# Phase one of a fused attention and MLP kernel: first norms deferred, fewer transposes on TensorE, x loads and attention outputs moved

## The chip, the cores and the metric

The kernel runs on one core of one Trainium2 chip. The metric is the device time of one execution in microseconds (us), as the median of several runs. Experiments ran beside runs of the kernel before. A ratio is the mean time of one kernel's fast runs over that of the other's fast runs of the same rounds, so it is not quite the ratio of the medians quoted. A profile is one execution; its span lies about 2 us below the time of the run it was taken in.

## The reference, cut to what matters

The input x is 2048 rows of 1024 values in bf16. It is normalised once, and two branches take the result: a memory-augmented attention (not touched here, apart from one number) and a mixer with an MLP.

```python
xn = _layernorm(x)                       # "first norm"
out = x + A(xn, ...) + B(xn, ...)
# B starts with a second norm of the same rows and a matmul:
h  = _gelu(_layernorm(xn) @ w1)          # phase one of the kernel
x1 = xn + shift(h) @ w2                  # phase two
h2 = _gelu(_layernorm(x1) @ w3) @ w4     # phase three
```

## The kernel before

Phase one works on 16 tiles of 128 rows. For each tile it needs the statistics of x (`norm_stats`: VectorE, then an inverse root on POOL, called the factor below), the second norm `xn2` (computed straight from x, bf16), its transpose `xn2T`, eight groups of matmuls with w1 (`stage1`), and a gelu on ScalarE per group. A group writes one of four PSUM buffers, and its gelu frees that buffer for a later group. The first norm `xn` is needed only later, by phase two and by the attention; it is kept in SBUF and also written to a scratch in HBM.

The order within each engine is the order of the program text; the PE timeline of the profile before shows it in tile 0's stage: six groups of eight matmuls from 8.38 us, half of tile 1's transpose at 11.77 us, one group at 12.06 us, the other half at 12.51 us. Tiles 0 to 7 are transposed by TensorE (matmuls with the identity, copied out of PSUM by ScalarE); tiles 8 to 15 are normalised on ScalarE and transposed by DMA. The core of the code, cut:

```python
NPE = 8
def norm2(n, xn2T, jj):
    ...
    if n < NPE:                                  # VectorE
        nc.vector.tensor_scalar(xn2, xts[n], mean, rstd2, op0=subtract, op1=mult)
    else:                                        # ScalarE, then a DMA transpose
        nc.scalar.activation(xn2, xts[n], Identity, bias=nm2, scale=rstd2)
        nc.sync.dma_start_transpose(xn2T[:, jj], xn2)

def norm1(n):                                    # first norm, and its write
    nc.vector.tensor_scalar(xn, xts[n], mean, rstd1, op0=subtract, op1=mult)
    nc.gpsimd.dma_start(xn_v[:, n, :], xn)       # to the scratch in HBM
    load_x(n + 10)                               # ten x buffers
    ...
for n in range(1, NPE):
    norm_stats(n + 1, 0); norm2_of(n); norm_stats(n + 1, 1)
    if n > 1: norm1(n - 2)                       # two tiles behind
    if n < 4: stage1(n - 1, 1, ..., transposes of tile n after groups 5 and 6)
...
def prep(n):                                     # tiles 8 to 15, inside stage1
    norm2_of(n); norm_stats(n + 1); norm1(n - 2)
for n0 in range(4, NT, 2):                       # two tiles at a time
    stage1(n0, 2, tiles2[n0], between)           # 256 columns per matmul
```

In the attention the outputs of a tile are put in the order of the program 12 us (in block 0) or 10 us (in blocks 1 to 4) of estimated TensorE time after its scores.

Of the kernel before, what the change touches and what calls it, by code (L numbers as in the profile page):

```python
# [15 lines left out]
BF16 = mybir.dt.bfloat16  # L16
F32 = mybir.dt.float32
# [6 lines left out]
P = 128  # L24
S = 2048
D = 1024
KT = D // P
NT = S // P
# [49 lines left out]
def kernel(  # L78
# [114 lines left out]
    with tc.manual_schedule(engines={mybir.EngineType.PE, mybir.EngineType.SP, mybir.EngineType.Pool}), ExitStack() as actx:  # L193
# [6 lines left out]
        with ExitStack() as bctx:  # L200
# [13 lines left out]
            with ExitStack() as hctx:  # L214
# [7 lines left out]
                with ExitStack() as p0:  # L222
                    big = p0.enter_context(tc.tile_pool(name="p0big", bufs=1))
                    ring = p0.enter_context(tc.tile_pool(name="p0ring", bufs=3))
                    w1_sb = big.tile([P, KT, D], BF16)
                    NPE = 8

                    xts = {}

                    def load_x(n):  # L230
                        if n < NT:
                            xts[n] = ring.tile([P, D], BF16, tag="xt", bufs=10, name=f"xt{n}")
                            nc.sync.dma_start(xts[n][:], x_v[:, n, :])

                    load_x(0)
# [5 lines left out]
                        load_x(n)  # L241
                    for i in range(4):
                        nc.sync.dma_start(w2_sb[:, 2 * i:2 * i + 2, :], w2_v[:, 2 * i:2 * i + 2, :])
                    for n in range(7, 10):
                        load_x(n)

                    stats = {}

                    def norm_stats(n, part=None):

                        if n >= NT:
                            return
                        xt = xts[n]
                        if n not in stats:
                            stats[n] = [ring.tile(shape, F32, tag=tag, bufs=6, name=f"{tag}{n}") for tag, shape in (("st", [P, 2, 6]), ("mv", [P, 2]), ("ab", [P, 2]), ("rr", [P, 2]), ("nm2", [P, 1]))]
                        st, mv, ab, rr, nm2 = stats[n]
                        if part in (None, 0):
                            nc.vector.bn_stats(st[:, 0, :], xt[:, 0:512])
                        if part == 0:
                            return  # L260
                        nc.vector.bn_stats(st[:, 1, :], xt[:, 512:1024])
                        nc.vector.bn_aggr(mv[:], st[:])
                        nc.vector.scalar_tensor_tensor(ab[:], epsm[:], mv[:, 1:2], epsa[:], op0=ALU.mult, op1=ALU.add)
                        nc.gpsimd.tensor_tensor(rr[:], ab[:], neghalf[:], op=ALU.pow)
                        if n >= NPE:
                            nc.gpsimd.tensor_scalar(nm2[:], mv[:, 0:1], rr[:, 1:2], -1.0, op0=ALU.mult, op1=ALU.mult)

                    def norm2(n, xn2T, jj):
                        st, mv, ab, rr, nm2 = stats[n]
                        xn2 = ring.tile([P, D], BF16, tag="xn2")  # L270
                        if n < NPE:
                            for c in (slice(0, 512), slice(512, 1024)) if n == 0 else (slice(0, 1024),):
                                nc.vector.tensor_scalar(xn2[:, c], xts[n][:, c], mv[:, 0:1], rr[:, 1:2], op0=ALU.subtract, op1=ALU.mult)
                        else:
                            nc.scalar.activation(xn2[:], xts[n][:], ACTF.Identity, bias=nm2[:], scale=rr[:, 1:2])
                            nc.sync.dma_start_transpose(xn2T[:, jj], xn2[:])
                        return xn2

                    def norm1(n):
                        st, mv, ab, rr, nm2 = stats[n]  # L280
                        xn = xn_keep[n // 4][:, n % 4]
                        nc.vector.tensor_scalar(xn, xts[n][:], mv[:, 0:1], rr[:, 0:1], op0=ALU.subtract, op1=ALU.mult)
                        nc.gpsimd.dma_start(xn_v[:, n, :], xn)
                        load_x(n + 10)
                        if n in (12, 15):
                            load_w3()
                        return xn
# [10 lines left out]
                    def stage1(n0, nt, xn2T, between, j0=0):  # L298
                        w = nt * P
                        for co in range(KT):  # L300
                            ps = psum.tile([P, 512], F32, tag="mm", bufs=4)
                            for k in range(KT):
                                nc.tensor.matmul(ps[:, :w].rearrange("p (n t) -> p n t", t=P), w1_sb[:, k, co * P:(co + 1) * P],  # L303
                                                 xn2T[:, j0:j0 + nt, k, :], start=(k == 0), stop=(k == KT - 1))
                            nc.scalar.activation(hTB[:, co, 2 + n0 * P:2 + n0 * P + w], ps[:, :w], ACTF.Gelu_apprx_tanh)
                            for f in between.get(co, ()):
                                f()
# [13 lines left out]
                    tiles2, xn2s = {}, {}  # L321

                    def norm2_of(n):
                        if n % 2 == 0:
                            tiles2[n] = xn2T_tile()
                        xn2s[n] = norm2(n, tiles2[n - n % 2], n % 2)

                    def tr(n, half, on_dve=False):
                        transposes(xn2s[n], tiles2[n - n % 2], n % 2, half, on_dve)
# [6 lines left out]
                    nc.gpsimd.memset(hTB[:, :, 0:2], 0.0)  # L336
                    nc.gpsimd.memset(hTB[:, :, S + 2:S + 4], 0.0)
                    load_consts(4)
                    for n in range(1, NPE):
                        if n > 1:  # L340
                            norm_stats(n + 1, 0)
                        norm2_of(n)
                        norm_stats(n + 1, 1 if n > 1 else None)
                        if n > 1:
                            norm1(n - 2)
                        if n < 4:
                            stage1(n - 1, 1, tiles2[(n - 1) // 2 * 2], {5: [lambda n=n: tr(n, 0)], 6: [lambda n=n: tr(n, 1)]}, (n - 1) % 2)
                    stage1(3, 1, tiles2[2], {4: [lambda: tr(4, 0)], 5: [lambda: tr(4, 1)], 6: [lambda: tr(5, 0)], 7: [lambda: tr(5, 1)]}, 1)

                    def prep(n):  # L350
                        norm2_of(n)
                        norm_stats(n + 1)
                        norm1(n - 2)

                    for n0 in range(4, NT, 2):
                        between = {c: [] for c in range(KT)}
                        if n0 + 4 < NT:
                            between[1 + 2 * (n0 == 4)] += [lambda n0=n0: prep(n0 + 4)]
                            between[4 + 2 * (n0 == 4)] += [lambda n0=n0: prep(n0 + 5)]
                        if n0 == 4:  # L360
                            for c in range(4):
                                between[1 + 2 * c // 2 + (c > 1)] += [lambda c=c: tr(6 + c // 2, c % 2)]
                        stage1(n0, 2, tiles2[n0], between)
                    for n in (NT - 2, NT - 1):
                        norm1(n)

                xn3T = [wpool.tile([P, 4, KT, P], BF16, tag="w", name=f"xn3T{tb}") for tb in range(4)]
                with ExitStack() as p2:
                    ring = p2.enter_context(tc.tile_pool(name="p2ring", bufs=4))
                    for n in range(NT):  # L370
                        x1 = ring.tile([P, D], F32, tag="x1")
                        st = ring.tile([P, 2, 6], F32, tag="st")
# [7 lines left out]
                        mv = ring.tile([P, 2], F32, tag="mv")  # L380
# [14 lines left out]
            with ExitStack() as p3:  # L395
# [3 lines left out]
                ring = p3.enter_context(tc.tile_pool(name="p3ring", bufs=2))  # L399
# [114 lines left out]
                for tb in range(4):  # L514
# [18 lines left out]
                    for j in range(4):  # L533
                        n = tb * 4 + j
# [223 lines left out]
        for gi_, group in enumerate(groups):  # L758
# [3 lines left out]
            for hg in range(8):  # L762
# [26 lines left out]
                for i, (B, t, QT, KTt, V) in enumerate(work):  # L789
                    due = clock[0] + 1.0 + i * step  # L790
                    if B["b"] not in oXs:
                        oXs[B["b"]] = oX_last if B["b"] == 4 else [abig.tile([P, H, 384], BF16, tag="oX", name=f"oX{B['b']}")]
                        if B["b"] == 3:
                            oXs[3].append(abig.tile([P, H, P], BF16, tag="oXb", name="oXb"))
                        oX_last = oXs[B["b"]]
                    j, at = divmod(480 if t["gi"] == 21 else t["tok"], 384)
                    oX = oXs[B["b"]][j]

                    def s_item(t=t, hg=hg, QT=QT, KTt=KTt, V=V, oX=oX, at=at, due=due, gi_=gi_):
                        PTr = scores(t, hg, QT, KTt)  # L800

                        def o_item():
                            outputs(t, hg, PTr, V, oX, at)
                            return 0.18
                        smalls.append((clock[0] + (12.0 if gi_ == 0 else 10.0), ("O", gi_), o_item))
                        return 0.18
                    smalls.append((due, ("S", gi_), s_item))
            outs = [Out(oXs[B["b"]], 3 * B["b"] + gl, gl, ch * 512) for B in Bs for gl in range(4 if B["b"] == 4 else 3) for ch in range(2)]
# [187 lines left out]
```

## Time and profile before

The median was 1521.8 us of 3 runs.

| what (profile before) | value |
|---|---|
| span | 1519.6 us |
| TensorE (PE) busy | 1508.8 us, 99% |
| TensorE waiting, all waits named | under 4 us |
| first matmul of phase two (L377) | at 69.39 us |
| granted TensorE clock | 1.00 from 6.9 us to 0.6 us before the end of the span |

First the page of the kernel before: the line of PE in the table of engines (busy time, share of the span, instructions), and the chain that ended last by engine.

```profile
PE 1508.8 (99%) x9781; PEld 808.3 (53%) x9853; DVE 546.2 (36%) x1137; ACT 506.7 (33%) x1147; POOL 179.4 (12%) x248
...
PE 98%; DMA 1%; issue 0%; DVE 0%; ACT 0%; SPq 0%; POOL 0%
```

Next all waits of PE in the kernel before: who waited for whom, us in total, how often, the longest.

```profile
PE warm L320 <- DVE wz L314: 1.4, 1, 1.4
PE ps L303 <- ACT xn2T L296: 0.5, 1, 0.5
PE psO L690 <- DMA PT<-Pn: 0.4, 1, 0.4
PE ps L292 <- DVE xn L273: 0.4, 1, 0.4
PE ps L651 <- DMA wt<-in_A_Wq_dram: 0.3, 1, 0.3
PE pso L709 <- issue: 0.2, 1, 0.2
```

There is hardly anything to win but TensorE's own instructions. No matmul of phase one waits for a DMA transpose (xn2T from DMA is not among the releasers; the one such wait, PT in the attention, is 0.4 us). The third view is the timeline of PE in phase one (start, duration, engine, line, operation, count):

```profile
32.49 0.39 PE L292 MATMUL ps<-c_ident_sb,xn 128*128 128x128 bf16 x4
32.71 36.84 PE L303 MATMUL ps<-xn2T,w_sb 128*128 128x256 bf16 x336
69.39 10.96 PE L377 MATMUL ps<-w_sb,hTB 128*128 128x512 bf16 x49
```

After the last transpose on TensorE (L292) phase one runs without a gap, 109 ns per matmul of 256 columns, until phase two begins.

### The profile page before, as it was taken

To read this page: it belongs to the slowest core of one execution; us is meant where nothing else is said; L and a number is where in the kernel's file an instruction comes from. 1 tells how busy PE (TensorE), PEld (TensorE's weight loads), DVE (VectorE), ACT (ScalarE), POOL (GpSimd) and SP (SyncE) were. 2 spreads that over 40 slices of the span, in tenths; PEclk is the share of its full clock that TensorE was granted. 3 is DMA by queue.
4 is the path that set the end of the run, shared out by engine and by line. 5 is a ranking of instruction groups with operands and counts; after the bars stand their busy time and mean duration, and the time that the engine had idled before them with its cause. 6 is when DMAs were issued, how large, how long until landed. Compare 5 with 4: busy or idle time off the path is not lost.

```text
span 1519.6 us, 24277 instructions
## 1 busy us (share of the span) xinstructions
PE 1508.8 (99%) x9781; PEld 808.3 (53%) x9853; DVE 546.2 (36%) x1137; ACT 506.7 (33%) x1147; POOL 179.4 (12%) x248
## 2 busy tenths in 40 slices
PE   9999999999999999999999999999999999999998
PEld 7844444445444444444466645654665555445555
DVE  7382230100120122222246614651664266416542
ACT  6533203013022011111256614650663266326630
POOL 5231020211111231100000010001000100010001
PEclk9999999999999999999999999999999999999999
DMA  8799762353355887532499947992997389628611
GB/s 283 157 266 317 220 174 93 136 201 111 126 169 141 198 281 255 192 133 70 137 240 253 238 117 189 244 238 79 228 240 190 118 223 217 185 76 209 175 46 53
DMA packets 306459, 274.20 MB, mean 180 GB/s; under 512 B 153787, under 2 KB 274128, under 8 KB 306088
## 3 DMA queue, kind: packets, MB, share of 16 engines
q1 hardware_dynamic: 284168, 189.92, 49.3%
q0 software_dynamic: 22032, 82.63, 15.9%
q8 instruction: 79, 1.29, 0.4%
q14 instruction: 36, 0.29, 0.1%
q10 hardware_dynamic: 144, 0.07, 0.0%
HBM read 190.98 MB, written 46.19 MB: 156 GB/s over the span
## 4 chain that ended last, share of the span: by engine, by line
PE 98%; DMA 1%; issue 0%; DVE 0%; ACT 0%; SPq 0%; POOL 0%
PE ps L651 30%; PE pso L709 14%; PE ps L577 14%; PE ps L519 13%; PE ps L545 13%; PE ps L377 4%; PE ps L303 3%; PE psS L666 2%; PE psO L690 2%; PE ps L836 1%; PE ps L469 1%; PE ps L434 0%; PE gps L448 0%; DMA wt<-in_A_Wq_dram 0%; DMA PT<-Pn 0%; PE warm L320 0%
## 5 line engine op out<-in xcount | busy, mean ns | idle before, releaser
L651 PE MATMUL ps<-hTb,wt 128*128 128x396 bf16 (+3 forms) x2528 | 500.4, 343 | 0.3 <-DMA wt<-in_A_Wq_dram 0.3
L651 PEld LDWEIGHTS <-wt 128*128 128x128 bf16 x2528 | 232.2, 98 | 167.6 <-DMA wt<-in_A_Wq_dram 0.7
L577 PE MATMUL ps<-wt,xT 128*128 128x512 bf16 x1003 | 220.1, 379 | 1.1
L709 PE MATMUL pso<-wo_sb,oX 128*128 128x512 bf16 x938 | 209.3, 379 | 1.2 <-issue 0.2
L519 PE MATMUL ps<-xn3T,w_sb 128*128 128x512 bf16 x896 | 196.2, 379 | 0.0
L545 PE MATMUL ps<-w_sb,h3T 128*128 128x512 bf16 x873 | 194.3, 379 | 1.2
L577 PEld LDWEIGHTS <-xT 128*128 128x128 bf16 x1024 | 100.2, 98 | 120.8
L520 ACT ACTIVATE h3T<-ps 128x512 bf16<-128x512 f32 x112 | 66.9, 597 | 290.4 <-PE ps L519 289.5
L709 PEld LDWEIGHTS <-oX 128*128 128x128 bf16 x960 | 92.6, 98 | 108.2
L657 ACT CAST KT<-ps 128x396 bf16<-128x396 f32 (+3 forms) x160 | 82.3, 514 | 186.9 <-PE ps L651 184.2
L545 PEld LDWEIGHTS <-h3T 128*128 128x128 bf16 x896 | 87.0, 98 | 103.4
L519 PEld LDWEIGHTS <-w_sb 128*128 128x128 bf16 x896 | 86.6, 98 | 102.1
L672 DVE TENSOR_REDUCE sums<-sm 99x4 f32<-99x396 f32 (+2 forms) x176 | 97.6, 555 | 113.0 <-ACT sm L670 113.0
L659 ACT ACTIVATE QT<-ps 128x396 bf16<-128x396 f32 (+3 forms) x160 | 84.2, 527 | 119.1 <-PE ps L651 102.0
L668 DVE TENSOR_TENSOR sm<-psS,c_mask_reg_sb 99x396 f32<-99x396 f32 x160 | 91.3, 571 | 86.3 <-PE psS L666 85.7
L579 ACT CAST Vs<-ps 128x512 bf16<-128x512 f32 x64 | 37.5, 587 | 233.1 <-PE ps L577 174.9
L670 ACT ACTIVATE sm<-sm 99x396 f32<-99x396 f32 (+2 forms) x176 | 92.9, 528 | 63.7 <-DVE sm L668 60.7
L583 DVE CAST Vs<-ps 128x512 bf16<-128x512 f32 x64 | 44.3, 692 | 170.0 <-PE ps L577 158.0
L678 DVE TENSOR_TENSOR Pn<-sm,rs 99x396 bf16<-99x396 f32 (+2 forms) x176 | 99.0, 562 | 7.2 <-DMA PT<-Pn 1.1
L546 DVE TENSOR_TENSOR R<-ps,R 128x512 f32<-128x512 f32 x32 | 21.9, 690 | 180.9 <-PE ps L545 166.6
L716 POOL DMA_DIRECT2D out_dram<-ot x30 | 16.4, 547 | 584.0 <-DVE ot L715 578.2
L715 DVE TENSOR_TENSOR ot<-pso,Rt 128x512 bf16<-128x512 f32 (+1 forms) x33 | 22.3, 676 | 172.3 <-PE pso L709 166.9
(120 smaller groups left out, 1072.0 us busy)
## 6 DMA issues: line engine op xcount, KB each, us to landing
wt<-in_A_Wq_dram SPq DMA_DIRECT2D x76, 512.0 KB
wt<-in_A_Wk_dram SPq DMA_DIRECT2D x76, 512.0 KB
wt<-in_A_Wv_dram POOLq DMA_DIRECT2D x24, 1024.0 KB, 6.5
V_scratch<-Vs SPq DMA_DIRECT2D x32, 512.0 KB
V<-V_scratch SPq DMA_DIRECT2D x32, 384.0 KB
R_scratch<-x POOLq DMA_DIRECT2D x16, 512.0 KB, 3.9
R<-R_scratch SPq DMA_DIRECT2D x16, 512.0 KB
R_scratch<-R POOLq DMA_DIRECT2D x16, 512.0 KB, 3.2
```

The lines of the kernel that those rows point to most:

```text
L519: nc.tensor.matmul(ps[:].rearrange("p (n t) -> p n t", t=P), w3_sb[:, k, f * P:(f + 1) * P], xn3T[tb][:, :, k, :], start=(k == 0), stop=(k ...
L520: nc.scalar.activation(h3T[:, f, :], ps[:], ACTF.Gelu_apprx_tanh)
L545: nc.tensor.matmul(ps[:], h3T[:, f, j * P:(j + 1) * P], w4_sb[:, f, ch * 512:(ch + 1) * 512], start=(f == 0), stop=(f == FT - 1))
L577: nc.tensor.matmul(ps[:], xT[:, m4 * 4 + j, k, :], wv[:, k, :], start=(k == 0), stop=(k == KT - 1))
L651: nc.tensor.matmul(ps[:, :nb] if flat else ps[:, :nb].rearrange("p (t c) -> p t c", t=nt), w[:, k, hh * P:(hh + 1) * P], B["rhs"](k), star ...
L657: nc.scalar.copy(o, i)
L659: nc.scalar.mul(o, i, scale)
L668: nc.vector.tensor_tensor(sm[:T, :, :T], S3, t["mask"][:].unsqueeze(1).to_broadcast((T, 4, T)), op=ALU.add)
L670: nc.scalar.activation(e[:T, :, :T], sm[:T, :, :T], ACTF.Exp, scale=LN2)
L672: nc.vector.tensor_reduce(ss, e[:T, :, :T], axis=AX.X, op=ALU.add)
L678: nc.vector.tensor_tensor(Pn[:T, :, :T], e[:T, :, :T], rs[:T, :].unsqueeze(2).to_broadcast((T, 4, T)), op=ALU.mult)
L709: nc.tensor.matmul(self.ps[:, :self.w], self.oX[self.gl // 3][:, h, self.gl % 3 * P:(self.gl % 3 + 1) * P], wo_sb[:, h, self.cc], start=(h ...
```

## The change

The intent: less work for TensorE (only tiles 0 to 4 are transposed there; 5 to 7 go to the DMA), earlier second norms for that (the first norms are put off and then done two per tile), x loads that are put off and issued together, ahead of the next tile's second norm and transpose, instead of one behind each first norm (and nine x buffers instead of ten, which leaves room for statistics that live longer), and outputs at 12 us in all blocks of the attention. The diff, cut to its core:

```diff
-                    NPE = 8
+                    NPE, NDVE = 5, 8
-            xts[n] = ring.tile([P, D], BF16, tag="xt", bufs=10, name=f"xt{n}")
+            xts[n] = ring.tile([P, D], BF16, tag="xt", bufs=9, name=f"xt{n}")
-                    for n in range(7, 10):
+                    for n in range(7, 9):
                         load_x(n)
 ...   # statistics: bufs=6 -> bufs=12; norm2 on VectorE for n < NDVE, DMA transpose for n >= NPE
                         nc.gpsimd.dma_start(xn_v[:, n, :], xn)
-                        load_x(n + 10)
+                        x_due.append(n + 9)
 ...
+                    def s_and_n(n):
+                        norm_stats(n + 1, 0); norm2_of(n); norm_stats(n + 1, 1)
+                    def more_x():
+                        while x_due: load_x(x_due.pop(0))
 ...   # trs(n, c): the two half transposes of tile n after groups c and c + 1
+                    s_and_n(2);  stage1(1, 1, tiles2[0], trs(2, 4), 1)
+                    s_and_n(3);  stage1(2, 1, tiles2[2], trs(3, 4))
+                    s_and_n(4);  s_and_n(5)
+                    stage1(3, 1, tiles2[2], trs(4, 4), 1)
+                    s_and_n(6);  norm1(0);  norm2_of(7);  norm_stats(8)
+                    stage1(4, 1, tiles2[4], {0: [more_x]})
+                    norm1(1);  norm1(2);  norm_stats(9)
                     def prep(n):
+                        more_x()
                         norm2_of(n)
-                        norm_stats(n + 1)
-                        norm1(n - 2)
+                        if n + 2 < NT: norm_stats(n + 2)
+                        for m in range(2*n - 13, 2*n - 11) if n < 12 else range(n - 1, n + n//15):
+                            norm1(m)
+                    stage1(5, 1, tiles2[4], {2: [prep(8)], 6: [prep(9)]}, 1)
+                    for n0 in range(6, NT, 2):
+                        stage1(n0, 2, tiles2[n0], {2: [prep(n0 + 4)], 5: [prep(n0 + 5)]} ...)
 ...
-    smalls.append((clock[0] + (12.0 if gi_ == 0 else 10.0), ("O", gi_), o_item))
+    smalls.append((clock[0] + 12.0, ("O", gi_), o_item))
```

More of the change, by code (lines that the diff above doesn't have):

```diff
@@ L254, in norm_stats @@
                         if n not in stats:
-                            stats[n] = [ring.tile(shape, F32, tag=tag, bufs=6, name=f"{tag}{n}") for tag, shape in (("st", [P, 2, 6]), ("mv", [P, 2]), ("ab", [P, 2]), ("rr", [P, 2]), ("nm2", [P, 1]))]
+                            stats[n] = [ring.tile(shape, F32, tag=tag, bufs=12, name=f"{tag}{n}") for tag, shape in (("st", [P, 2, 6]), ("mv", [P, 2]), ("ab", [P, 2]), ("rr", [P, 2]), ("nm2", [P, 1]))]
                         st, mv, ab, rr, nm2 = stats[n]
@@ L264, in norm_stats @@
                         nc.gpsimd.tensor_tensor(rr[:], ab[:], neghalf[:], op=ALU.pow)
-                        if n >= NPE:
+                        if n >= NDVE:
                             nc.gpsimd.tensor_scalar(nm2[:], mv[:, 0:1], rr[:, 1:2], -1.0, op0=ALU.mult, op1=ALU.mult)
@@ L270, in norm2 @@
                         xn2 = ring.tile([P, D], BF16, tag="xn2")
-                        if n < NPE:
+                        if n < NDVE:
                             for c in (slice(0, 512), slice(512, 1024)) if n == 0 else (slice(0, 1024),):
@@ L275, in norm2 @@
                             nc.scalar.activation(xn2[:], xts[n][:], ACTF.Identity, bias=nm2[:], scale=rr[:, 1:2])
+                        if n >= NPE:
                             nc.sync.dma_start_transpose(xn2T[:, jj], xn2[:])
                         return xn2
+                    x_due = []
                     def norm1(n):
@@ L338 @@
                     load_consts(4)
-                    for n in range(1, NPE):
-                        if n > 1:
-                            norm_stats(n + 1, 0)
+                    def s_and_n(n):
+                        norm_stats(n + 1, 0)
                         norm2_of(n)
-                        norm_stats(n + 1, 1 if n > 1 else None)
-                        if n > 1:
-                            norm1(n - 2)
-                        if n < 4:
-                            stage1(n - 1, 1, tiles2[(n - 1) // 2 * 2], {5: [lambda n=n: tr(n, 0)], 6: [lambda n=n: tr(n, 1)]}, (n - 1) % 2)
@@ L348, with trs @@
-                    stage1(3, 1, tiles2[2], {4: [lambda: tr(4, 0)], 5: [lambda: tr(4, 1)], 6: [lambda: tr(5, 0)], 7: [lambda: tr(5, 1)]}, 1)
+                        norm_stats(n + 1, 1)
+                    def more_x():
+                        while x_due:
+                            load_x(x_due.pop(0))
+                    def trs(n, c):
+                        return {c: [lambda: tr(n, 0)], c + 1: [lambda: tr(n, 1)]}
+                    norm2_of(1)
+                    norm_stats(2)
+                    stage1(0, 1, tiles2[0], trs(1, 5))
@@ new lines @@
+                    s_and_n(2)
+                    stage1(1, 1, tiles2[0], trs(2, 4), 1)
+                    s_and_n(3)
+                    stage1(2, 1, tiles2[2], trs(3, 4))
+                    s_and_n(4)
+                    s_and_n(5)
+                    stage1(3, 1, tiles2[2], trs(4, 4), 1)
+                    s_and_n(6)
+                    norm1(0)
+                    norm2_of(7)
+                    norm_stats(8)
+                    stage1(4, 1, tiles2[4], {0: [more_x]})
+                    norm1(1)
@@ L350, in prep @@
+                    norm1(2)
+                    norm_stats(9)
                     def prep(n):
+                        more_x()
                         norm2_of(n)
-                        norm_stats(n + 1)
-                        norm1(n - 2)
-                    for n0 in range(4, NT, 2):
-                        between = {c: [] for c in range(KT)}
-                        if n0 + 4 < NT:
-                            between[1 + 2 * (n0 == 4)] += [lambda n0=n0: prep(n0 + 4)]
-                            between[4 + 2 * (n0 == 4)] += [lambda n0=n0: prep(n0 + 5)]
-                        if n0 == 4:
-                            for c in range(4):
-                                between[1 + 2 * c // 2 + (c > 1)] += [lambda c=c: tr(6 + c // 2, c % 2)]
-                        stage1(n0, 2, tiles2[n0], between)
@@ L364 @@
-                    for n in (NT - 2, NT - 1):
-                        norm1(n)
+                        if n + 2 < NT:
+                            norm_stats(n + 2)
+                        for m in range(2 * n - 13, 2 * n - 11) if n < 12 else range(n - 1, n + n // 15):
+                            norm1(m)
+                    stage1(5, 1, tiles2[4], {2: [lambda: prep(8)], 6: [lambda: prep(9)]}, 1)
+                    for n0 in range(6, NT, 2):
+                        stage1(n0, 2, tiles2[n0], {2: [lambda n0=n0: prep(n0 + 4)], 5: [lambda n0=n0: prep(n0 + 5)]} if n0 + 4 < NT else {})
```

## The prediction

> **What bounds the kernel.** TensorE. The engine table has PE busy 1508.8 of 1519.6 us, the chain of waits is 98% PE, and the windows view has PE at 19.8 us or more of every 20 us but the first, the last and 780 to 800. The granted clock is 1.00. The waits view gives PE under 4 us of waiting: 1.4 before the warm-up, 0.5 + 0.4 at phase one's start, 0.4 (a late probability transpose) and 0.3 (a late Wq) in block 0. So only less TensorE work or those stalls can move the time: tenths of a per cent.
>
> **TensorE's work** (instruction order of both kernels, starts from the timeline):
> - Tiles 5, 6, 7 are transposed by DMA, not TensorE: 24 matmuls go, 56 ns each from start to start: -1.34 us.
> - Tiles 4 and 5 run singly: 128 matmuls of 128 columns (56 ns) for 64 of 256 (109 ns): +0.19 us.
> - Transposes of tiles 2 to 4 come one channel group earlier. Before, the next tile's fifth matmul waited 0.17 us for ScalarE's copy (three times), and the first 256-column group 0.24 us: -0.7 us. But tile 2's transpose now comes up near 15.6 us, and its normalised input is ready near 15.85: +0.3 us.
> Sum: -1.6 us, if nothing new stalls.
>
> **New waits.** Without first norms between them VectorE's cycle per tile falls from 2.72 to about 2.5 us (it then waits for POOL's root, 1.06 us from input to use). Estimated from these: second norm of tile 5 done near 23.3 us, 7 near 28.2. A DMA transpose took about 3 us from issue to its last packets. So tile 5 lands near 26.5 (needed near 29), tile 7 near 31.3 (needed near 33). Tile 8's second norm is on ScalarE inside a single-tile stage, waits for its factor until 31.3 us and takes 1.24 us; four PSUM buffers at 0.45 us hide less: 0.3 to 0.6 us of stall. Tile 9's transpose stands behind two x loads that wait for VectorE; it lands near 40 us, just when needed: 0 to 1 us. I expect 0.8 us eaten. [...]
>
> **Outputs later (12 for 10).** In blocks 1 to 4 no psO matmul waits before the change (the late one is in block 0, which had 12 already). The same matmuls are only reordered. Worth 0; at block ends and in the tail within 0.3 us either way.
>
> First norms later are off the path (needed from 69 us); VectorE, ScalarE and POOL have slack from 45 us.
>
> **Predicted:** 1520.9 us, 0.9 us less; 8 in 10 between 1519.6 and 1522.2. Faster by over 2%: 0.01, within 2%: 0.98, slower by over 2%: 0.01.
>
> **What would show it.** Phase two's first matmul starts at 69.4 us now; it should start 0.5 to 1.7 us earlier, later stages shift by the same with unchanged lengths. Transposing matmuls go from 64 to 40. PE waits on tile 2's second norm (0.3 us) and on ScalarE near 32 us. Output matmuls in blocks 1 to 4 show no wait before or after; block 0's two waits stay.
>
> **What would make it wrong.** A DMA transpose landing several us late (loads fill the DMA to 22 us), stalling TensorE at tile 5, 7 or 9; other alignment of block 0's loads (about 1 us); or output matmuls that wait in unprofiled runs, so that 12 saves more.

## The result, and the profile after

The changed kernel took 1530.15 us (6 runs, 1527.32 to 1533.3); the kernel before took 1521.55 us (6 runs, 1520.96 to 1522.35). The ratio is 1.0055, interval 1.0042 to 1.0068. So it is slower by 8.6 us in the medians, outside the predicted range. Its runs also scatter by 6 us instead of 1.4.

The same two lines of the page of the changed kernel:

```profile
PE 1511.1 (99%) x9821; PEld 808.9 (53%) x9893; DVE 546.0 (36%) x1137; ACT 503.5 (33%) x1149; POOL 177.2 (12%) x248
...
PE 94%; DMA 3%; DVE 1%; issue 0%; SPq 0%; POOL 0%; ACT 0%; ACTq 0%
```

PE is busy for longer, although its instructions should take 1.15 us less (the first two terms of the forecast, -1.34 and +0.19 us), and DMA and DVE have come onto the chain. The waits of PE, as before (L306 is `stage1`, L308 its gelu):

```profile
PE ps L306 <- DMA xn2T<-xn: 7.2, 2, 4.4
PE ps L306 <- ACT hTB L308: 2.1, 2, 1.8
PE warm L323 <- DVE wz L317: 1.4, 1, 1.4
PE ps L669 <- DMA wt<-in_A_Wq_dram: 0.5, 1, 0.5
PE ps L306 <- ACT xn2T L299: 0.5, 1, 0.5
PE ps L295 <- DVE xn L273: 0.4, 1, 0.4
PE psO L708 <- DMA PT<-Pn: 0.2, 1, 0.2
```

Two waits on DMA transposes and two on the gelu are new, 9.3 us together. The timeline of PE in the changed kernel says where they are; the bracket gives the idle time before and who ended it:

```profile
32.62 3.23 PE L306 MATMUL ps<-xn2T,w_sb 128*128 128x128 bf16 x32 [0.31 <-ACT hTB L308]
37.62 4.53 PE L306 MATMUL ps<-xn2T,w_sb 128*128 128x256 bf16 x40 [1.77 <-ACT hTB L308]
46.57 9.50 PE L306 MATMUL ps<-xn2T,w_sb 128*128 128x256 bf16 x64 [4.42 <-DMA xn2T<-xn]
58.86 22.47 PE L306 MATMUL ps<-xn2T,w_sb 128*128 128x256 bf16 x192 [2.78 <-DMA xn2T<-xn]
81.16 0.38 PE L395 MATMUL ps<-w_sb,hTB 128*128 128x512 bf16 x1
```

Phase two starts at 81.16 us instead of 69.39, 11.8 us later, in a profiled run that took 1533.3 us (the slowest of the six). The part after it has not changed: from the start of phase two to the start of the last matmul it is 1445.8 us after and 1446.1 us before. The whole loss lies in phase one.

The group at 46.57 us waited for tile 9, the group at 58.86 us for tile 11. There is a second thing in these lines: 64 matmuls of 256 columns took 9.50 us, or 148 ns each; before, each took 109 ns. The view by windows shows why. Its columns are the stretch, its length, PE's busy time and matmul count, the granted clock, the share of the DMA engines and GB/s:

```profile
core 0: us, PE busy (x), PEclk, DMA share, GB/s
38.00:42.00 4.00, 4.00 (x39) 1.00 0.79 215
42.00:46.50 4.50, 0.15 (x2) 0.79 1.05 208
46.50:51.50 5.00, 4.93 (x24) 0.51 1.13 201
51.50:56.00 4.50, 4.50 (x42) 1.00 1.15 246
56.00:58.80 2.80, 0.08 (x1) 0.90 1.14 178
58.80:61.70 2.90, 2.84 (x14) 0.51 1.06 398
```

After each of the two long gaps the clock is halved: the clock records give 0.5 from 44.58 us for 6.83 us and from 58.23 us for 3.41 us, and the matmuls in those times start 213 ns apart instead of 109. Of that time 4.8 and 2.8 us held matmuls, so half of 7.6 us, 3.8 us, was lost on top of the gaps. How much idle time came before each half clock is told in the last section.

The sum for the profiled run: 9.3 us of waits, plus 3.8 us of half clock, less the 1.7 us that the change saved where no such wait was left (e11, below), is 11.4 us of the 11.8 measured.

Two questions remain: why the transposes of tiles 9 and 11 came late, and why the gelus did. The queue of SP (DMA issues, transposes and loads in order) and the second norms on ScalarE in the changed kernel:

```profile
29.75 1.54 SPq L233 DMA_DIRECT2D xt<-in_A_x_dram  x3
32.44 1.43 SPq L277 DMA_TRANSPOSE xn2T<-xn  x1
37.15 0.80 SPq L233 DMA_DIRECT2D xt<-in_A_x_dram  x2
38.05 1.24 SPq L277 DMA_TRANSPOSE xn2T<-xn  x1
```

```profile
31.17 1.24 ACT L275 ACTIVATE xn<-xt,nm,rr 128x1024 bf16<-128x1024 bf16 x1 [0.33 <-POOL nm L266]
36.17 1.24 ACT L275 ACTIVATE xn<-xt,nm,rr 128x1024 bf16<-128x1024 bf16 x1 [3.10 <-POOL nm L266]
```

```profile
33.19 0.69 DVE L258 BATCH_NORM_STATS2 st<-xt 128x6 f32<-128x512 bf16 x1 [2.53 <-DMA xt<-in_A_x_dram]
```

The load of x9 now has to wait for first norm 0 (nine buffers; it ended at 26.92 us) and for tile 7's transpose ahead of it in the queue (its issue lasted from 28.07 to 29.69 us); it is issued at 29.75 us. VectorE stands 2.53 us for it (third fence), tile 9's factor is late, and ScalarE, whose next instruction is tile 9's second norm, stands 3.10 us (second fence) with gelus behind it. ScalarE ran in the order of the program here: TensorE had finished four groups by 35.85 us, but their gelus start only at 37.32 us, behind that norm (36.17 us). Until then no PSUM buffer comes free, and TensorE stands 1.77 us. Tile 9's transpose is issued only at 38.05 us.

But it then took until 45.2 us, and TensorE was released only when the last of the transpose's 16 semaphore updates came: they lie between 45.66 and 46.53 us, and TensorE went on at 46.57 us. The DMA packet records of the trace tell more: each transpose is 1024 packets of 256 bytes on queue 1, and each write of an xn tile to the scratch is 64 packets of 4096 bytes on queue 0. This table, made from those records, gives the time from the first to the end of the last packet of each transpose, and in brackets how many write packets started in that time:

| tile | 8 | 9 | 10 | 11 | 12 | 13 |
|---|---|---|---|---|---|---|
| before | 1.70 (15) | 1.98 (37) | 2.50 (71) | 4.09 (94) | 2.41 (92) | 1.74 (38) |
| changed | 2.08 (61) | 5.56 (112) | 6.04 (180) | 4.07 (142) | 1.52 (34) | 1.42 (5) |

The table counts packets alone. The last semaphore update came 1.3 us after tile 9's last packet in the changed kernel and 0.6 us after it in a run without writes (e8, below). And writes are not needed to stretch a transpose: tile 15 of the kernel before took 3.54 us with none of them, beside 61 packets of a weight load.

In the kernel before, the writes of the first six tiles had gone out before the first DMA transpose. In the changed kernel all 16 come after 28 us and, two per tile, fall on the transposes of tiles 8 to 11, which TensorE is waiting for. That gives two theories: W, the bunched writes stretch the transposes; X, the late x loads delay everything. A rival to both is that the later outputs of the attention cost time.

### The profile page after: what moved, and what is told of

Same layout as the page of the kernel before. It is cut to its first block, busy times and chain, and to the rows that moved or that the text cites. A ratio compares the mean times of both kernels' runs of the same rounds, so it can differ in the third digit from the quotient of the medians.

```text
span 1531.5 us, 24357 instructions
## 1 busy us (share of the span) xinstructions
PE 1511.1 (99%) x9821; PEld 808.9 (53%) x9893; DVE 546.0 (36%) x1137; ACT 503.5 (33%) x1149; POOL 177.2 (12%) x248
## 4 chain that ended last, share of the span: by engine, by line
PE 94%; DMA 3%; DVE 1%; issue 0%; SPq 0%; POOL 0%; ACT 0%; ACTq 0%
PE ps L669 29%; PE pso L727 14%; PE ps L595 14%; PE ps L537 13%; PE ps L563 13%; PE ps L395 4%; PE psS L684 2%; PE psO L708 2%; PE ps L306 1%; DMA xn2T<-xn 1%; DMA wt<-in_A_Wq_dram 1%; DMA xt<-in_A_x_dram 1%; PE ps L854 1%; PE ps L487 1%; DMA PT<-Pn 1%; PE gps L466 0%
## 5 line engine op out<-in xcount | busy, mean ns | idle before, releaser
L669 PE MATMUL ps<-hTb,wt 128*128 128x396 bf16 (+3 forms) x2528 | 494.7, 343 | 0.6 <-DMA wt<-in_A_Wq_dram 0.5
L537 PE MATMUL ps<-xn3T,w_sb 128*128 128x512 bf16 x896 | 196.2, 379 | 0.0
L537 PEld LDWEIGHTS <-w_sb 128*128 128x128 bf16 x896 | 86.6, 98 | 102.1
```

Of the source, the lines that this page charges most:

```text
L537: nc.tensor.matmul(ps[:].rearrange("p (n t) -> p n t", t=P), w3_sb[:, k, f * P:(f + 1) * P], xn3T[tb][:, :, k, :], start=(k == 0), stop=(k ...
L669: nc.tensor.matmul(ps[:, :nb] if flat else ps[:, :nb].rearrange("p (t c) -> p t c", t=nt), w[:, k, hh * P:(hh + 1) * P], B["rhs"](k), star ...
```

## The experiments

All twelve gave right results. In the table "before" is the median of the kernel before on the same chip; the ratio is to it.

| run | us | before | ratio (interval) |
|---|---|---|---|
| changed kernel | 1530.15 | 1521.55 | 1.0055 (1.0042 to 1.0068) |
| e1_out10 | 1533.27 | 1521.62 | 1.0079 (1.0062 to 1.0096) |
| e2_out12_alone | 1520.59 | 1521.57 | 0.9992 (0.9979 to 1.0006) |
| e3_writes_late | 1546.42 | 1521.62 | 1.0158 (1.0141 to 1.0175) |
| e4_x10 | 1529.32 | 1521.62 | 1.0057 (1.0040 to 1.0074) |
| e5_both | 1543.31 | 1521.62 | 1.0147 (1.0128 to 1.0167) |
| e6_keep_warm | 1531.07 | 1521.57 | 1.0058 (1.0042 to 1.0073) |
| e7_norms_back | 1524.69 | 1521.57 | 1.0028 (1.0008 to 1.0048) |
| e8_writes_end | 1522.99 | 1521.57 | 1.0004 (0.9989 to 1.0020) |
| e9_writes_end_x10 | 1520.90 | 1521.26 | 0.9999 (0.9983 to 1.0014) |
| e10_norms_back | 1521.04 | 1521.26 | 0.9999 (0.9983 to 1.0014) |
| e11_repaired | 1519.24 | 1521.26 | 0.9989 (0.9975 to 1.0003) |
| e12_before_pairs | 1526.69 | 1521.26 | 1.0038 (1.0023 to 1.0054) |

### The later outputs: e1 and e2

The changed kernel with the old delay, and the old kernel with the new delay:

```diff
 # e1, against the changed kernel (e2 is the reverse, in the kernel before)
-    smalls.append((clock[0] + 12.0, ("O", gi_), o_item))
+    smalls.append((clock[0] + (12.0 if gi_ == 0 else 10.0), ("O", gi_), o_item))
```

> The changed kernel with only the outputs' delay put back (12 in block 0, 10 elsewhere). If the loss lies in phase one, as the comparison of the traces says (phase two's first matmul at 81.2 us instead of 69.4, everything after it of equal length to 0.3 us): the time stays at 1528 to 1532 us. If the later outputs cost the time in the attention blocks (rival): it falls to about 1520 to 1523 us.

> The kernel before with only the outputs later in all blocks (12 everywhere). The profile before has no output matmul waiting in blocks 1 to 4, and the attention part of both profiles was of equal length to 0.3 us: ratio 0.9995 to 1.0005. If later outputs helped or hurt in unprofiled runs: over 1 us apart.

e1 stayed slow (four runs, 1529.7 to 1534.6 us), so the outputs are not what costs. e2's interval holds 1; its median is 1 us lower, which does not decide whether later outputs win anything.

### Writes moved into phase two: e3 (and e5 with ten x buffers)

```diff
 # norm1, phase one
-                        nc.gpsimd.dma_start(xn_v[:, n, :], xn)
 # phase two, in the loop over tiles
                         nc.gpsimd.tensor_scalar(nm3[:], mv[:, 0:1], r3[:], ...)
+                        nc.gpsimd.dma_start(xn_v[:, n, :], xn_keep[n // 4][:, n % 4])
```

> The changed kernel with the 16 writes of xn to its scratch moved from phase one into phase two, the first norms themselves where they are. Theory W (the writes, which now come in pairs, share the DMA engines with the transposes of tiles 9 to 11 and stretch them from about 1.5 us to 4 to 6 us): each transpose takes 1.4 to 2.5 us from first to last packet, TensorE's waits of 4.4 and 2.8 us on the transposes shrink to under 1.5 us together, the clock stays at 1.0 after warm-up, time about 1521 to 1523 us. Theory X (the loads of x9 and later come too late, because nine buffers and the queue's order hold them back; the writes are harmless): no change, 1528 to 1532 us. The 1.8 us wait on ScalarE near 36 us should stay in either.

> Both repairs together: writes of xn in phase two, ten x buffers. If lateness and stretching are the whole loss, no wait of TensorE over 0.6 us is left in phase one, phase two starts at 67.5 to 68.5 us (69.4 before the change), time 1519.5 to 1521 us, faster than both kernels by a little over the kernel before. If something else in the change costs time, it stays above 1522 us.

Both totals missed both theories by far. The waits of PE in e3 say where the time went (L394 is phase two's matmul, L537 phase three's):

```profile
PE ps L537 <- ACT h3T L538: 12.7, 1, 12.7
PE ps L394 <- DVE x L395: 11.3, 3, 7.0
...
PE ps L305 <- DMA xn2T<-xn: 1.0, 1, 1.0
```

In phase one the edit did what W said: the waits on transposes fell from 7.2 to 1.0 us, tiles 9 to 11 took 2.60, 0.94 and 0.94 us, and phase two began at 70.73 us. Phase two, which writes R1 at 512 KB per tile and transposes its own tiles, could not bear the writes: 24.0 us of waits in phases two and three came in their place (the first two lines). Why exactly was not followed up: as a test of W's total the place was badly chosen. In e5, with ten buffers, phase two began at 69.00 us (67.5 to 68.5 expected), with one wait of 0.76 us on a transpose.

### Ten x buffers: e4

```diff
-   xts[n] = ring.tile([P, D], BF16, tag="xt", bufs=9, name=f"xt{n}")
+   xts[n] = ring.tile([P, D], BF16, tag="xt", bufs=10, name=f"xt{n}")
-                    for n in range(7, 9):
+                    for n in range(7, 10):
-                        x_due.append(n + 9)
+                        x_due.append(n + 10)
 # room for it: three buffers instead of twelve for the statistics that are used at once
```

> The changed kernel with ten x buffers and x9 loaded in front, as before the change (smaller rings for three statistics make the room). Theory X: VectorE no longer waits 2.5 us for x9, ScalarE no longer stands 3.1 us for tile 9's factor, TensorE's 1.8 us wait on ScalarE goes to under 0.5, and tile 9's transpose starts near 34 to 35 us instead of 38, so the 4.4 us wait goes too: time about 1520 to 1523 us. Theory W alone: the ScalarE wait goes, the transposes of tiles 9 to 11 still take 4 to 6 us, waits on them of 2 us or more stay, time 1524 to 1529 us.

The timeline of PE in e4:

```profile
32.98 7.61 PE L306 MATMUL ps<-xn2T,w_sb 128*128 128x128 bf16 x72 [0.32 <-ACT hTB L308]
44.62 29.40 PE L306 MATMUL ps<-xn2T,w_sb 128*128 128x256 bf16 x256 [4.04 <-DMA xn2T<-xn]
```

The 1.77 us wait on the gelu is gone, as X said, but the wait on tile 9 is still 4.04 us, and the median did not improve measurably. (The profiled run, at 1526.8 us, was the fastest of four.) Both theories missed a part. Against X, tile 9's transpose was issued at 37.28 us, not at 34 to 35: its norm was done at 35.15 us, but two x loads stood ahead of it in the queue and were issued at 36.38 us. So this run does not remove all of the lateness. Against W, the transposes of tiles 9 to 11 took 3.41, 2.40 and 3.10 us, not 4 to 6; the wait stayed because tile 9's last semaphore update came at 44.48 us, 1.9 us after its last packet. What settles the matter is e8 below, where tile 9's transpose was issued just as late.

### Keeping TensorE busy in the gaps: e6

```diff
+  def keep_warm(k):                                     # k matmuls of zeros
+      ps = psum0.tile([P, 4, P], F32, tag="tr")
+      for i in range(k):
+          nc.tensor.matmul(ps[:].rearrange("p a b -> p (a b)"), wz[:, :P], wz[:], ...)
   for n0 in range(6, NT, 2):
+      if n0 in (8, 10): keep_warm(20 if n0 == 8 else 12)
       stage1(n0, 2, ...)
```

> The changed kernel with 20 matmuls of zeros (4.3 us) ahead of the group that waits for tile 9's transpose and 12 (2.6 us) ahead of the one that waits for tile 11's; nothing else. If the half clock after a gap is a cost of its own (in the changed kernel's profile the granted clock was 0.5 for 6.8 and 3.4 us, 7.6 us of which held matmuls: 3.8 us): clock 1.0 throughout, the group after the gap at 109 ns per 256 columns instead of 213, time 2 to 4 us below the changed kernel's 1530, near 1527 us. If the clock fell for another reason than the gap: still 0.5 there, no gain.

No gain. The timeline of PE in e6:

```profile
38.28 6.19 PE L306 MATMUL ps<-xn2T,w_sb 128*128 128x256 bf16 x40 [2.32 <-ACT hTB L308]
44.52 4.26 PE L385 MATMUL ps<-wz 128*128 128x512 bf16 x19
48.62 7.15 PE L306 MATMUL ps<-xn2T,w_sb 128*128 128x256 bf16 x64
```

After the dummies the clock stayed at 1.0: the 64 matmuls of tile pair 8 took 7.15 us instead of 9.50. But this time the wait on the gelu was 2.32 us, and that gap alone brought the half clock from 38.71 us for 3.41 us, so that the 40 matmuls before the dummies took 6.19 us instead of 4.53. And the dummies ran to 48.8 us, while tile 9's transpose had been complete at 46.30 us (its last semaphore update). The 2.35 us that they saved in clock they cost in time (2.3 us). In this run matmuls in the gap kept the clock up; the run doesn't give the clock's share in the total. The clock's share rests on the clock records and the starts of matmuls above.

### First norms back in their old places: e7 and e10

```diff
 # e7, against the changed kernel
   def s_and_n(n):
       norm_stats(n + 1, 0); norm2_of(n); norm_stats(n + 1, 1)
+      norm1(n - 2)
-  s_and_n(6); norm1(0); norm2_of(7); norm_stats(8)
+  s_and_n(6); norm2_of(7); norm_stats(8); norm1(5)
-  norm1(1); norm1(2)
-  for m in range(2*n - 13, 2*n - 11) if n < 12 else range(n - 1, n + n//15):   # in prep
+  for m in range(n - 2, n - 1 + 2*(n // 15)):
 # e10 adds, in s_and_n, ahead of norm2_of(n):
+      more_x()
```

> The changed kernel with the first norms back in their old places (each two tiles behind its second norm, so their writes to the xn scratch fall one by one from 17 us on); five tiles on TensorE, nine x buffers and the x loads' places as changed. Theory D (the deferral does the harm: it bunches the writes in pairs on the transposes of tiles 9 to 11, 112 to 180 write packets per transpose against 15 to 94 before): transposes take 1.4 to 4 us, phase two starts by 72 us, time 1520 to 1524 us. Theory X (late x loads): x9 still comes behind tile 7's transpose, the ScalarE stall near 36 us stays and the time is 1526 us or more.

> The changed kernel with the first norms back in their old places and the loads of x9 to x12 ahead of tile 5's and 6's transposes: of the change only the five tiles on TensorE, nine buffers and later outputs are left. If deferral and the place of the x loads are the whole loss: no ScalarE stall over 0.6 us, transposes of 1.4 to 3 us, time 1520.5 to 1522.5 us. If moving tiles 5 to 7 from TensorE to DMA costs by itself (their transposes now meet the writes of the first norms): waits on the transposes of tiles 5 to 7, 1523 us or more.

e7 gave back 5.5 of the 8.6 us, a little less than D expected. Phase two began at 72.72 us in its profile (72 expected). What was left were gelu waits of 1.4 and 1.7 us and 1.3 us on a transpose; with the late x9 out of the way as well (e10), only one of them stayed. e10, with the loads also in front, was level with the kernel before; there one gelu wait of 1.33 us stayed, against an expected 0.6, and no wait on any transpose. So five tiles on TensorE, nine buffers and later outputs do no harm by themselves that these runs resolve. The deferral and the place of the x loads do.

### Writes at the end of phase one: e8, and with ten buffers: e9

```diff
 # norm1
-                        nc.gpsimd.dma_start(xn_v[:, n, :], xn)
 # after the last stage1
+                    for i in range(4):
+                        nc.sync.dma_start(xn_v[:, 4 * i:4 * i + 4, :], xn_keep[i][:])
```

> The changed kernel with the writes of xn to scratch as four large ones at the end of phase one, behind its last transpose on the same queue. The earlier run with the writes in phase two had the transposes short (0.9 to 2.6 us) and phase two started at 70.7 us instead of 81.2, but phase two then paid for the writes, so its total said nothing. Theory W: phase two starts near 70 to 71 us (the ScalarE stall of 1.4 to 1.8 us is left) and, if these four writes hinder nothing, the time is 1521 to 1523.5 us. If phase two or three pay again, its first matmul is early but later phases are longer.

> The changed kernel with both repairs, the writes of xn at the end of phase one (as in the run that gave 1523.0 us) and ten x buffers. Each repair is to take its own share: the ScalarE stall of 1.4 us goes, too, phase two starts at 69 to 69.5 us and the time is 1521 to 1522 us, level with the kernel before. If the buffers did nothing more: 1523 us.

The timeline of PE in e8, where the first norms are still deferred and the x loads still late:

```profile
37.29 4.53 PE L305 MATMUL ps<-xn2T,w_sb 128*128 128x256 bf16 x40 [1.35 <-ACT hTB L307]
42.78 28.12 PE L305 MATMUL ps<-xn2T,w_sb 128*128 128x256 bf16 x256 [0.97 <-DMA xn2T<-xn]
70.74 9.44 PE L397 MATMUL ps<-w_sb,hTB 128*128 128x512 bf16 x42
```

Compare with the changed kernel: the wait on tile 9 is 0.97 us instead of 4.42, the one on tile 11 is gone, the clock stays at 1.0 (256 matmuls in 28.12 us are 110 ns each), and phase two starts at 70.74 us. This recovers 7.2 of 8.6 us in the medians. The transposes of tiles 8 to 11 took 1.82, 2.52, 0.94 and 0.94 us with no write beside them. Tile 9's transpose was issued at 37.73 us, nearly as late as in the changed kernel (38.05), and was complete at 42.73 us instead of 46.53: so it is not the late issue that cost most. e9 removed the gelu wait of 1.35 us too and came out level with the kernel before. e8 also changed the issuing engine and the size of the writes, so by itself it does not show that the bunching was at fault; the next one does.

### The converse: the kernel before with writes in pairs, e12

```diff
 # norm1, in the kernel before
-                        nc.gpsimd.dma_start(xn_v[:, n, :], xn)
+                        held.append(n)
 # prep(n), n = 8 to 15
                         norm2_of(n); norm_stats(n + 1); norm1(n - 2)
+                        write_pair()      # issues up to two of the writes that are held
```

> The converse: the kernel before, with nothing changed but that the 16 writes of xn are held and issued in pairs from tile 8's preparation on, as the deferral does; all norms, loads and transposes where they were. Theory W: the transposes of tiles 8 to 11, 1.7 to 4.1 us before, stretch to 4 to 6 us, TensorE waits on them for 2 us or more in all, time 1523.5 to 1530 us. If the writes are not what stretches the transposes (but the order of the x loads, which is left alone here): 1521 to 1522.5 us, no waits.

The timeline of PE in e12:

```profile
32.23 15.96 PE L310 MATMUL ps<-xn2T,w_sb 128*128 128x256 bf16 x144
49.13 7.15 PE L310 MATMUL ps<-xn2T,w_sb 128*128 128x256 bf16 x64 [0.94 <-DMA xn2T<-xn]
59.38 15.80 PE L310 MATMUL ps<-xn2T,w_sb 128*128 128x256 bf16 x128 [3.10 <-DMA xn2T<-xn]
75.01 5.34 PE L387 MATMUL ps<-w_sb,hTB 128*128 128x512 bf16 x23
```

Nothing but the writes was moved, and the old kernel shows the disease of the new one: 5.4 us slower, waits of 0.94 and 3.10 us on transposes, and a half clock of 3.41 us from 60.06 us. The transposes of tiles 11, 12 and 13 took 4.55, 5.86 and 4.31 us with 170, 293 and 152 write packets beside them, against 4.09, 2.41 and 1.74 us before. The expectation had named tiles 8 to 11; it was 11 to 13, because in this kernel the writes piled up later.

### A repaired version: e11

e9, and the second norms of tiles 8 and 9 on VectorE, so that no gelu stands behind a norm that waits:

```diff
-                    NPE, NDVE = 5, 8
+                    NPE, NDVE = 5, 10
                     def prep(n):
                         more_x()
-                        norm2_of(n)
+                        if n != 9: norm2_of(n)
+                        if n == 8: norm2_of(9)
```

> Both repairs, and the second norms of tiles 8 and 9 on VectorE instead of ScalarE (ScalarE serves its queue in order, so a norm that waits for its factor holds the gelus behind it and with them the PSUM buffers). Counted from the first transposing matmul, phase two started after 62.1 us before the change; TensorE's work is 1.15 us less and the copies' waits another 0.5 us, so with waits under 0.6 us left it is 60.6 to 61.4 us here, time 1520 to 1521 us: faster than both kernels, by 0.5 to 1.5 us. If waits of 1 us or more stay: 1521.5 us or more.

That ScalarE serves its queue in order is what the changed kernel's trace shows (3.10 us of standing for tile 9's factor, four gelus behind the norm, 1.77 us of TensorE).

The timeline of PE in e11:

```profile
24.75 43.14 PE L305 MATMUL ps<-xn2T,w_sb 128*128 128x128 bf16 x464
67.72 12.47 PE L400 MATMUL ps<-w_sb,hTB 128*128 128x512 bf16 x55
```

From 24.75 us on phase one has no gap. Counted from the first transposing matmul, phase two starts after 60.35 us, against 62.07 us before: the 1.7 us that the change was after, and a little better than the 60.6 to 61.4 us expected. The median is 1519.24 us, 2.0 us below the kernel before on the same chip, but one of five runs was at 1521.86 us, and the interval of the ratio (0.9975 to 1.0003) just holds 1. It clearly beats the changed kernel; that it beats the kernel before is likely and not proven.

## Why the prediction was wrong

- **The bound.** Right. TensorE bounds the kernel, and only its work and its waits moved the time.
- **TensorE's work, -1.6 us.** Right as a mechanism: where the waits were removed (e11), phase one was 1.7 us shorter.
- **Tile 2's transpose, +0.3 us.** About right: in the profiles with the new place the wait on its second norm was 0 to 0.2 us.
- **"A DMA transpose took about 3 us from issue to its last packets."** This is the step that failed. It fits the first two DMA transposes of the trace before (3.0 and 3.2 us), which had 15 and 37 write packets beside them. The fourth, in the same trace, took 5.6 us. For tile 9 the changed kernel needed 7.2 us, for tile 11 11.2 us, where the first norms' writes came in pairs. Of tile 11's 11.2 us, 7.1 went by before its first packet: its issue lasted 4.34 us instead of 1.24, and its packets began at 53.60 us, as those of tile 10 ended (53.81). The prediction counted the deferred first norms as "off the path" because their result is needed late. Their writes were on it, as load on the DMA engines.
- **"Tile 9 ... 0 to 1 us", "I expect 0.8 us eaten".** Measured in the profiled run: 4.42 us on tile 9, 2.78 us on tile 11, which was not in the sum at all.
- **The stall on ScalarE, "0.3 to 0.6 us".** The mechanism was right (tile 9's rather than tile 8's second norm, in order with the gelus); the size was 0.31 + 1.77 us, because the estimate had x9 in time and VectorE waited 2.53 us for it.
- **The clock.** Missing from the sum. Gaps of 4.42 and 2.78 us cost another 3.8 us at half clock, so the 7.2 us of waits on the transposes must be priced at about half as much again. It may explain part of the scatter, as the mean granted clock of the six runs lies between 0.996 and 0.999; only one of them has a trace that could show it.
- **Outputs at 12, worth 0.** Not contradicted: e1 and e2 show no effect that the runs resolve.
- **"What would make it wrong"** named transposes landing late and TensorE stalling at tile 5, 7 or 9. It was tile 9, and tile 11.

What stays open: why packets last longer beside those of other transfers. At the packets' usual durations (medians: 18 ns for the transposing packets, 159 for the writes, 84 for the x loads) tile 9's transpose with 112 writes and 78 load packets comes to about 2.7 us per engine if all 16 share evenly (64 x 18 + 7 x 159 + 5 x 84 ns); it took 5.56 us. In that time the mean durations were 40, 277 and 174 ns, and with those the same sum is 5.4 us: the engines were occupied nearly all the time, by packets that lasted longer.

## What to carry to other kernels

When work is put off because its result is not needed yet, ask also what it sets off: here a deferred norm carried a write to HBM, and two of those per tile landed on the transfers that TensorE was waiting for. Take the cost of a DMA from the trace under the load that it will meet, not from its quietest occurrence. On a kernel bound by TensorE, count a gap of more than about 2 us with the half clock that may follow it (here it followed gaps of 2.32, 2.78, 3.10 and 4.42 us, not one of 3.04 us, and none of 1.77 us or less), and keep anything that waits (a norm, a factor) out of an in-order queue that also frees PSUM buffers (here it cost TensorE 1.77 us).

## What the traces show of gaps and of transposes

- Gaps and the clock, after the warm-up. Gaps of TensorE of 2.32 (e6), 2.78 (changed kernel) and 3.10 us (e12) brought a half clock of 3.41 us, and one of 4.42 us (changed kernel) a half clock of 6.83 us, while one of 3.04 us (e3, phase two) brought none: the 16 matmuls behind it took 3.61 us, as did the 16 behind a gap of 1.26 us. None of 1.77 us or less brought any. What fits the changed kernel's trace is how much of a gap fell into one period: every clock record but the last lasts a whole number of periods of 3.41 us (11, 2, 2, 1 and 430), and the clock fell at the end of full-speed periods with 2.43 us (of the gap of 4.42 us) and 2.16 us (of the gap of 2.78 us) of idle TensorE, and not of the one that held the whole gap of 1.77 us. The 3.04 us of e3 were, by its clock records, split over two periods, 1.40 and 1.64 us.
- How long a DMA transpose becomes beside other transfers: from its first to its last packet 0.94 to 2.52 us without writes (e8), 3.54 us beside a weight load (tile 15 before), and up to 6.04 us with 180 write packets of 4096 bytes (tile 10 of the changed kernel).
- The time from issue to data for a transpose of 128 x 1024 bf16 from SBUF to SBUF: 2.6 us to the last packet on a quiet DMA (tile 12 of e8), of which 1.24 us is the issue, and 3.05 us to the last semaphore update. Tile 14 of the kernel before and tile 15 of the changed one, without writes too, took 2.59 and 2.60 us to the last packet and 3.07 us to the last update.
